# Batch 0 of an attention and MoE kernel: other key orders in two query chunks, earlier splits of the next z, and stores of empty rows behind a later block

## The chip, the core and the metric

The kernel runs on one core of one Trainium2 chip. The metric is the device time of one execution in microseconds (us), of which the median of several runs counts. The core has five engines that run their own instruction streams: PE (TensorE, matmuls), DVE (VectorE), ACT (ScalarE), POOL (GpSimd) and SP (SyncE, which here only issues DMAs). An instruction waits for others through semaphores, and all that stands behind a waiting instruction on its engine waits with it.

## The reference

First an attention without softmax over 8 batches of 1856 rows, then a mixture of 16 experts (4 groups of 4) over all 14848 rows; each row goes to the one expert that the logits choose.

```python
scores = scale * np.matmul(z, z.transpose(0, 2, 1))      # z: (8, 1856, 64), scale = 1/1856
attn = np.maximum(scores, 0.0) ** 2
out = np.matmul(attn, v)                                 # v: (8, 1856, 256)
x = (u * out).reshape(8 * 1856, 256)
...
g_idx = np.argmax(x @ w_group, axis=1)                   # then e_idx in that group
h = np.maximum(xg[mask_e] @ w1[g, e], 0.0)               # 256 -> 1024
out[tok_idx] = combined[:, None] * (h @ w2[g, e])        # 1024 -> 256
```

## The kernel before, in words

**Attention.** The queries of a batch are cut into four chunks (c = 0 to 3) of 512, 512, 512 and 320, the keys into 15 tiles of 128 (the last has 64). A step `s` is one (batch, chunk, i); `key(b, c, i)` says which key tile it takes, by the table `KORD` (in batch 0 chunk 0 simply `i`). A value is carried as a high and a low part, so a product is two or three matmuls. A step computes scores for one key tile (L371, L372: two matmuls into `sc`), ACT makes `r` of them (L375 relu, L382 square), DVE splits `r` into `ah` and `al` (L383, L386), and six matmuls (L409, tiles `o`) add it to the output: for each of two halves of the model dimension ah by vl, ah by vh, al by vh. Scores run six steps ahead of these products. The first scores of a chunk need `zm`, the chunk's queries, which in batch 0 and for (1, 0) DVE copies from the split z (L272, L273).

**Mirrored tiles.** The scores are symmetric. Where a key tile belongs to an earlier chunk's columns, its `r` has been transposed by DVE into a tile `mt` (L311), stored to DRAM by SP (`sym<-mt`, L319), and comes back as `at` (`at<-sym`, L327, in `load_mirror`, 12 or so steps ahead of its key); such a step has no score matmuls, only `ah`, `al` from `at` (L360, L361). In batch 0 these are keys 4 to 7 in chunk 2 and keys 4 to 11 in chunk 3.

**The next batch's inputs.** z and v of batch 1 are loaded and split during batch 0, at the steps that `PREP0` names: for each piece (chunk, i) of the load and (chunk, i) of the split. A split of z is an ACT cast `z2h` (L249) and a DVE subtraction `z2l` (L256) of the loaded `zr`; of v, `vh` and `vl` (L294, L295).

**Chunk end.** When a chunk's products are done, DVE multiplies them by u into `xT` (L431), ACT and DVE split that into `xh` and `xl` (L437, L442), PE makes the logits `pl` (L484, L485: four matmuls), SP transposes the rows (`rows<-pl`, L472). Rows that hold no token are stored from `padrow` into the experts' buckets (L979 for all experts during batch 0; L972 in `fill` later).

**Buffers.** `r`, `ah`, `al`, `mt`, `zr`, `z2h`, `z2l` all take turns in one pool of 31 buffers; `vr`, `vh`, `vl`, `xh`, `xl` in another of 18. A tile that takes a buffer waits for the last reader of what was in it, which can be a DMA. `zm` has 2 buffers, `at` 3, `y` 3.

**Order.** From step 15 on, PE, ACT and DVE run in the order in which the program is written; SP and POOL are ordered by the scheduler.

**Experts.** The first four experts are worked off in blocks 0 to 11 of gathered rows (`xp` loaded by SP, L784; `xf` L798, `xh_m` L803, `xl_m` L804; hidden products L819 to L821; `hh` L824, `hl` L830; second product L904; `yr` L917; `y` L943, L946 on DVE; POOL scatters y to the output, L947). After a block, `FILL` says for which experts the stores of 768 empty rows are issued by SP (L972). The other 12 experts follow in pairs, which the change leaves alone.

Of the kernel before, what the change touches and what calls it, by code (L numbers as in the profile page):

```python
# [29 lines left out]
def tile_glu_attn_moe(  # L30
# [307 lines left out]
    def key(b, c, i):  # L338
        if (b, c) == (B - 1, NQ - 1):
            return (0, 1, 12, 2, 3, 14, 4, 5, 13, 6, 7, 8, 9, 10, 11)[i]  # L340
        return KORD[c][i] if b or c else i

    NS = len(steps)
# [4 lines left out]
    def scores(s):  # L348
        b, c, i = steps[s]
        k = key(b, c, i)  # L350
        w = QW[b][c]
        for far in (ATL, 12):
            lb, lc, li = steps[min(s + far, NS - 1)]
            lk = key(lb, lc, li)
            if lk % KT == 0 and mirrored(lb, lc, lk) and ((lc, lk) == (3, 8) and lb < B - 1) == (far != ATL):
                load_mirror(lb, lk // KT, KB[lc])
# [37 lines left out]
    def attn_v(s):  # L394
        b, c, i = steps[s]
        k = key(b, c, i)
        vh, vl = bv[(b, k // 4)]
        if i == 0:
            oacc[s] = [bank(ps_o, "o", f"o_{b}_{c}_{d}") for d in range(ND)]
        oa = oacc[s - i]  # L400
        end = i == NK - 1
        ah, al = hl.pop(s)
        prods = [(d, q) for d in range(ND) for q in range(3 if al is not None else 2)]
        if s < 2:
            prods.sort(key=lambda x: x[1] == 2)
        held = pin if s < NK else same
        for d, q in prods:
            d0 = (k % 4) * D + d * P
            held(nc.tensor.matmul(  # L409
                oa[d][:, 0:QW[b][c]], (vh if q else vl)[:, d0:d0 + P], al if q == 2 else ah,  # L410
                start=(i == 0 and q == 0), stop=end and q == (1 if al is None else 2),
            ))
# [555 lines left out]
    def fill(j):  # L968
        regs(j)
        n = 512 if j >= NOLD else 768  # L970
        at = nc.sync.value_load(sti[0:1, j:j + 1], min_val=512, max_val=(NE - 1) * CAPB + N)
        nc.sync.dma_start(  # L972
            views[NMARK + j][ds(at, n), :].rearrange("(p t) w -> p t w", p=P),
            padrow.unsqueeze(1).to_broadcast([P, n // P, RW]),
        )
# [22 lines left out]
    if B == 1:  # L998
# [2 lines left out]

    prep = {}
    PREP0 = (
        ("v", 0, (0, 13), (1, 7)), ("v", 1, (1, 1), (1, 11)), ("v", 2, (1, 5), (1, 14)), ("v", 3, (2, 4), (3, 2)), ("z", 0, (2, 4), (3, 4)), ("z", 1, (2, 10), (3, 6)), ("z", 2, (3, 0), (3, 9)), ("z", 3, (3, 1), (3, 12)),
    )
    PREP = (
        ("v", 0, (0, 3), (0, 11)), ("v", 1, (2, 0), (2, 9)), ("v", 2, (2, 3), (2, 13)), ("v", 3, (2, 6), (2, 14)),
# [19 lines left out]
    for s in range(NS):  # L1027
        b, c, k = steps[s]
# [46 lines left out]
    def more_rows(i):  # L1075
        if not (deferred or gens):
            while late["loaded"] < min(NB, i + 2):
                load_rows(late["loaded"])
                late["loaded"] += 1
# [327 lines left out]
        return hs, [lambda g=g, m=m: step(g, m) for g, m in seq]  # L1407

    unsent = []
    FILL = {1: (0, 1), 2: (2, 3), 7: (4, 5)}  # L1410
    x = xs[0]
    for i, (e, r0, n) in enumerate(blocks):
        if i == 0:
# [38 lines left out]
        more_rows(i)  # L1452
        for j in FILL.get(i, ()):
            fill(j)
# [180 lines left out]
```

## Time and profile before

| | us |
|---|---|
| median of 3 runs | 1425.8 (1424.71 to 1426.95) |
| the profiled execution's own time | 1420.93 |
| its span, first to last instruction | 1419.2 |
| PE busy in it | 1407.8 (99%) |
| DVE busy | 1217.8 (86%) |
| ACT busy | 1046.3 (74%) |
| POOL busy | 435.9 (31%) |

The profiled execution is 4.87 us under the median of the runs; sums made against it are carried over to the median. The mean granted TensorE clock was 0.999. A time in the trace counts from the first instruction. In the timeline a row gives start, duration, engine, line, operation, output and inputs, and in brackets how long the engine was idle before it and what ended that. Ends of matmuls are modelled, and matmuls overlap in the pipeline, so their pace is read from start to start. On SP (shown as SPq) a row is the time that the issuing took, not the transfer.

### The profile page before, as it was taken

To read this page: it belongs to the slowest core of one execution; us is meant where nothing else is said; L and a number is where in the kernel's file an instruction comes from. 1 tells how busy PE (TensorE), PEld (TensorE's weight loads), DVE (VectorE), ACT (ScalarE), POOL (GpSimd) and SP (SyncE) were. 2 spreads that over 40 slices of the span, in tenths; PEclk is the share of its full clock that TensorE was granted. 3 is DMA by queue.
4 is the path that set the end of the run, shared out by engine and by line. 5 is a ranking of instruction groups with operands and counts; after the bars stand their busy time and mean duration, and the time that the engine had idled before them with its cause. 6 is when DMAs were issued, how large, how long until landed. Compare 5 with 4: busy or idle time off the path is not lost.

```text
span 1419.2 us, 22637 instructions
## 1 busy us (share of the span) xinstructions
PE 1407.8 (99%) x6986; PEld 1216.1 (86%) x6986; DVE 1217.8 (86%) x2433; ACT 1046.3 (74%) x1836; POOL 435.9 (31%) x460
## 2 busy tenths in 40 slices
PE   9999999999999999999999999999999999999998
PEld 7888888888888888888887898988888888899997
DVE  8989989899999999999988668789777788888884
ACT  8878787787877878878776354357777777777773
POOL 0002112220222112202223231332445555555554
PEclk9999999999999999999999999999999999999999
DMA  7888969989899799897976576635655555566652
GB/s 237 241 198 226 247 164 253 239 196 232 190 260 234 178 250 208 223 242 158 251 189 170 143 197 146 121 84 143 144 152 129 145 145 134 138 153 152 154 141 59
DMA packets 402411, 257.78 MB, mean 182 GB/s; under 512 B 243827, under 2 KB 356238, under 8 KB 402288
## 3 DMA queue, kind: packets, MB, share of 16 engines
q1 hardware_dynamic: 390384, 225.29, 65.6%
q0 software_dynamic: 11824, 30.90, 7.8%
q8 instruction: 55, 0.90, 0.3%
q14 instruction: 68, 0.56, 0.1%
q10 hardware_dynamic: 80, 0.13, 0.0%
HBM read 110.65 MB, written 88.33 MB: 140 GB/s over the span
## 4 chain that ended last, share of the span: by engine, by line
PE 88%; DVE 4%; issue 3%; DMA 3%; POOL 1%; ACT 1%; SPq 0%; POOLq 0%; DVEq 0%; ACTq 0%
PE o L409 38%; PE duo_p L904 15%; PE duo_y L1359 6%; PE sc L371 4%; PE sc L372 4%; PE yT L904 4%; PE duo_w L1359 2%; PE duo_x L1359 2%; PE duo_p L1359 2%; PE duo_z L1359 2%; PE ph L819 2%; PE ph L820 2%; PE ph L821 2%; DMA out_dram<-y_w,meta_w 1%; PE pl L485 1%
## 5 line engine op out<-in xcount | busy, mean ns | idle before, releaser
L409 PE MATMUL o<-ah,vl 128*128 128x512 f32 (+1 forms) x960 | 354.9, 370 | 0.5 <-DVE ah L383 0.4
L409 PE MATMUL o<-ah,vh 128*128 128x512 f32 (+1 forms) x960 | 354.4, 370 | 0.0
L409 PE MATMUL o<-al,vh 128*128 128x512 f32 (+1 forms) x896 | 328.8, 370 | 0.8 <-DVE al L361 0.8
L647 POOL DMA_INDIRECT bucket<-rows,di x120 | 133.8, 1115 | 386.0 <-issue 216.6
L375 ACT ACTIVATE r<-sc 128x512 f32<-128x512 f32 (+1 forms) x300 | 172.8, 576 | 79.7 <-PE sc L372 70.5
L409 PEld LDWEIGHTS o<-ah,vl 128*128 128x128 f32 x960 | 180.3, 188 | 32.2 <-DVE ah L383 1.1
L409 PEld LDWEIGHTS o<-ah,vh 128*128 128x128 f32 x960 | 180.3, 188 | 29.9
L947 POOL DMA_INDIRECT out_dram<-y_w,meta_w x92 | 139.1, 1512 | 190.4 <-ACT y_w L941 145.4
L386 DVE TENSOR_TENSOR al<-r,ah 128x512 fp32r<-128x512 f32 (+1 forms) x268 | 181.1, 676 | 15.9 <-DVE ah L383 0.5
L409 PEld LDWEIGHTS o<-al,vh 128*128 128x128 f32 x896 | 167.9, 188 | 28.3 <-DVE al L361 1.1
L904 PE MATMUL duo_p<-hh_w,duo_w 128*128 128x496 f32 (+10 forms) x692 | 177.9, 371 | 0.0
L382 ACT ACTIVATE r<-r 128x512 f32<-128x512 f32 (+1 forms) x266 | 163.8, 616 | 8.5
L904 PEld LDWEIGHTS duo_p<-hh_w,duo_w 128*128 128x128 f32 x692 | 128.6, 188 | 16.7
L383 DVE CAST ah<-r 128x512 fp32r<-128x512 f32 (+1 forms) x266 | 110.4, 415 | 18.8 <-ACT r L382 9.8
L371 PE MATMUL sc<-zm,z2h 128*128 128x512 f32 (+1 forms) x300 | 116.2, 387 | 1.5 <-DVE zm L273 0.9
L372 PE MATMUL sc<-zm,z2l 128*128 128x512 f32 (+1 forms) x300 | 114.9, 383 | 0.0
L311 DVE STREAM_TRANSPOSE mt<-r 128x512 f32<-128x512 f32 x157 | 110.8, 706 | 0.7
L904 PE MATMUL duo_p<-hl_w,duo_w 128*128 128x496 f32 (+10 forms) x346 | 104.2, 371 | 0.0
L361 DVE TENSOR_TENSOR al<-at,ah 128x512 fp32r<-128x512 f32 (+1 forms) x180 | 101.8, 578 | 2.7 <-ACT ah L360 2.6
L360 ACT CAST ah<-at 128x512 fp32r<-128x512 f32 (+1 forms) x180 | 91.8, 530 | 5.9 <-DMA at<-sym 3.1
L824 ACT ACTIVATE hh<-ph 128x512 fp32r<-128x512 f32 (+6 forms) x96 | 45.4, 487 | 39.6 <-PE ph L821 38.9
L904 PE MATMUL yT<-hh,w_e 128*128 128x512 f32 (+6 forms) x352 | 73.9, 328 | 0.0
(263 smaller groups left out, 2876.1 us busy)
## 6 DMA issues: line engine op xcount, KB each, us to landing
sym<-mt SPq DMA_DIRECT2D x134, 256.0 KB
duo_r<-in_w_dram SPq DMA_DIRECT2D x48, 512.0 KB
at<-sym SPq DMA_DIRECT2D x88, 256.0 KB
bucket<-padrow SPq DMA_DIRECT2D x28, 528.0 KB
at<-sym SPq DMA_DIRECT2D x92, 160.0 KB
ut<-in_uT_dram SPq DMA_DIRECT2D x24, 512.0 KB
vr<-in_v_dram SPq DMA_DIRECT2D x23, 512.0 KB
raw_e<-in_w_dram SPq DMA_DIRECT2D x16, 512.0 KB
```

Source lines behind the costliest of these rows:

```text
L311: nc.vector.transpose(out=t2.rearrange("p (j t x) -> p t j x", t=KT, x=32), in_=a.rearrange("p (t j x) -> p t j x", t=KT, x=32))
L371: held(nc.tensor.matmul(ps[:, 0:w], z2h[:, ks], zm, start=True, stop=False))
L372: held(nc.tensor.matmul(ps[:, 0:w], z2l[:, ks], zm, start=False, stop=True))
L375: held(nc.scalar.activation(out=a, in_=ps[:, 0:w], func=AF.Relu, scale=1.0 / S))
L382: held(nc.scalar.activation(out=a, in_=a, func=AF.Square))
L383: held(nc.vector.tensor_copy(out=ah, in_=a))
L386: held(nc.vector.tensor_sub(out=al, in0=a, in1=f32(ah)))
L409: held(nc.tensor.matmul(oa[d][:, 0:QW[b][c]], (vh if q else vl)[:, d0:d0 + P], al if q == 2 else ah, start=(i == 0 and q == 0), stop=end a ...
L647: nc.gpsimd.indirect_dma_start(out=views[(b * NQ + 2 * half + hs[h]) * NT + i], out_offset=bass.IndirectOffsetOnAxis(ap=di[0:n, i0 + i:i0 ...
L904: nc.tensor.matmul(o, wt["2"][f // 2][:, w0:w0 + P], hs[f][q // 2][:, c0:c0 + n], start=(at == 0), stop=(at == 3 * NF - 1))
L947: nc.gpsimd.indirect_dma_start(out=outs(), out_offset=bass.IndirectOffsetOnAxis(ap=meta[0:m, t, 1:2], axis=0), in_=y[0:m], in_offset=None, ...
L1359: nc.tensor.matmul(out, a, b, start=(q == 0 and m in (1, 5)), stop=(q == 2), skip_group_check=True)
```

## The change

Two lines are added in `key`, and two tables of numbers change. In batch 0 the third chunk (c = 2) and the fourth (c = 3) get key orders of their own, in which the mirrored keys are spread differently among the others. The loads and splits of batch 1's four z pieces move earlier. The stores of empty rows for the experts 2 and 3 go from behind block 2 to behind block 5. Line numbers behind L341 rise by 2 in the changed kernel.

```diff
     def key(b, c, i):
...
+        if b == 0 and c > 1:
+            return ((12, 0, 4, 13, 1, 14, 5, 2, 3, 6, 8, 9, 7, 10, 11), (0, 4, 1, 5, 2, 6, 12, 7, 3, 13, 14, 8, 9, 10, 11))[c - 2][i]
         return KORD[c][i] if b or c else i
...
     PREP0 = (
-        ... ("z", 0, (2, 4), (3, 4)), ("z", 1, (2, 10), (3, 6)), ("z", 2, (3, 0), (3, 9)), ("z", 3, (3, 1), (3, 12)),
+        ... ("z", 0, (1, 12), (2, 5)), ("z", 1, (2, 4), (2, 11)), ("z", 2, (2, 8), (3, 4)), ("z", 3, (2, 9), (3, 9)),
     )
...
-    FILL = {1: (0, 1), 2: (2, 3), 7: (4, 5)}
+    FILL = {1: (0, 1), 5: (2, 3), 7: (4, 5)}
```

Before, batch 0 used `KORD[2] = (12, 0, 13, 1, 14, 2, 8, 3, 9, 4, 10, 5, 11, 6, 7)` and `KORD[3] = (0, 1, 2, 3, 12, 4, 5, 6, 7, 13, 14, 8, 9, 10, 11)`.

**Where the rows of chunk 1 are transposed (SP).** The third chunk's last two mirrored stores (`sym_0_2_3<-mt_0_2_13` and `..._14`) stand there among stores of empty rows (`bucket<-padrow`) and loads. The kernel before:

```order
L472 DMA_TRANSPOSE rows_0_0_548<-pl_0_0_550 128x4x128 x4
L319 DMA sym_0_2_3_756<-mt_0_2_13_806 128x512
L979 DMA bucket_69<-padrow_70 512x1x264
L319 DMA sym_0_2_3_756<-mt_0_2_14_841 64x512
L979 DMA bucket_69<-padrow_70 512x1x264 x2
```

The changed kernel:

```order
L474 DMA_TRANSPOSE rows_0_0_548<-pl_0_0_550 128x4x128 x4
L981 DMA bucket_69<-padrow_70 512x1x264
L244 DMA zr_1_0_807<-in_zT_dram 128x512
L319 DMA sym_0_2_3_761<-mt_0_2_13_819 128x512
L981 DMA bucket_69<-padrow_70 512x1x264
L319 DMA sym_0_2_3_761<-mt_0_2_14_856 64x512
L981 DMA bucket_69<-padrow_70 512x1x264
```

One store of empty rows and the load of `zr_1_0` now stand ahead of the store of `mt_0_2_13`.

**What waits for that store (ACT, and behind it DVE).** On ACT in the kernel before, `r_40` takes the buffer of `mt_0_2_13` and waits for its store:

```order
L375 ACTIVATE r_38_918<-sc_38_915 128x512
L382 ACTIVATE r_38_918<-r_38_918 128x512
L360 CAST ah_39_935<-at_0_1_2_791 128x512
L375 ACTIVATE r_40_952<-sc_40_949 128x512
L382 ACTIVATE r_40_952<-r_40_952 128x512
```

In the changed kernel `z2h_1_0` takes that buffer, and stands behind `r_40` (ACT):

```order
L377 ACTIVATE r_40_947<-sc_40_944 128x512
L384 ACTIVATE r_40_947<-r_40_947 128x512
L249 CAST z2h_1_0_960<-zr_1_0_807 128x512
L377 ACTIVATE r_41_970<-sc_41_967 128x512
L384 ACTIVATE r_41_970<-r_41_970 128x512
```

On DVE of the changed kernel `z2l_1_0` of this cast stands between `al_40` and the fourth chunk's `zm_0_3`:

```order
L385 CAST ah_40_949<-r_40_947 128x512
L388 TENSOR_TENSOR al_40_952<-r_40_947,ah_40_949 128x512
L256 TENSOR_TENSOR z2l_1_0_961<-zr_1_0_807,z2h_1_0_960 128x512
L272 CAST zm_0_3_964<-z2h_0_3_305 64x320
L273 CAST zm_0_3_964<-z2l_0_3_306 64x320
```

So the copies into `zm_0_3` now stand behind the split of z that waits for the store.

**The last products ahead of batch 1's first scores (PE).** `sc_60` is the first score of batch 1; `xl_0_2`, which the logits and a chain on DVE need, takes the buffer of a v piece that a product of chunk 3 reads last. In the kernel before that is `vl_0_0`, read last by step 48, five steps of products ahead of the logits:

```order
L409 MATMUL o_0_3_1_1142<-ah_48_1090,vl_0_0_186 128x320
L409 MATMUL o_0_3_1_1142<-ah_48_1090,vh_0_0_185 128x320
L409 MATMUL o_0_3_1_1142<-al_48_1093,vh_0_0_185 128x320
L371 MATMUL sc_55_1221<-zm_0_3_963,z2h_0_3_305 128x320
L372 MATMUL sc_55_1221<-zm_0_3_963,z2l_0_3_306 128x320
```

In the changed kernel it is `vl_0_1` (keys 4 to 7), read last by step 52, whose key is 7:

```order
L411 MATMUL o_0_3_1_1146<-ah_52_1153,vl_0_1_257 128x320
L411 MATMUL o_0_3_1_1146<-ah_52_1153,vh_0_1_256 128x320
L411 MATMUL o_0_3_1_1146<-al_52_1154,vh_0_1_256 128x320
L411 MATMUL o_0_3_0_1145<-ah_53_1180,vl_0_0_186 128x320
L411 MATMUL o_0_3_0_1145<-ah_53_1180,vh_0_0_185 128x320
L411 MATMUL o_0_3_0_1145<-al_53_1183,vh_0_0_185 128x320
L411 MATMUL o_0_3_1_1146<-ah_53_1180,vl_0_0_186 128x320
L411 MATMUL o_0_3_1_1146<-ah_53_1180,vh_0_0_185 128x320
L411 MATMUL o_0_3_1_1146<-al_53_1183,vh_0_0_185 128x320
L486 MATMUL pl_0_2_1298<-xh_0_2_1163,whl_85 48x512
L487 MATMUL pl_0_2_1298<-xl_0_2_1164,wh0_86 48x512
```

Behind these come the other two logits and `sc_60`. Between the last read of that buffer and `sc_60` there now stand eight products (two of step 52, six of step 53) and four logits on PE; before, these were two products of step 48, two scores, the steps 49 to 53 and four logits. On DVE, fifteen instructions from the first `xl_0_2` to the second `zm_1_0` stand there before as after, the same but for `z2l_1_2` in place of `z2l_1_0`.

## Rows read from the trace of the kernel before

**Rows 1.** The page: busy time of each engine, share of the span, instructions.

```profile
PE 1407.8 (99%) x6986; PEld 1216.1 (86%) x6986; DVE 1217.8 (86%) x2433; ACT 1046.3 (74%) x1836; POOL 435.9 (31%) x460
```

**Rows 2.** Timeline of PE, 79 to 80.4 us: start, duration, instruction, idle before it.

```profile
79.02 0.39 PE L409 MATMUL o<-ah,vh 128*128 128x512 f32 x1
79.25 0.39 PE L409 MATMUL o<-al,vh 128*128 128x512 f32 x1
80.14 0.38 PE L371 MATMUL sc<-zm,z2h 128*128 128x320 f32 x1 [0.51 <-DVE zm L273]
```

**Rows 3.** Timeline of SP's DMA issues, 62 to 92 us.

```profile
67.17 6.23 SPq L472 DMA_TRANSPOSE rows<-pl  x4
73.50 0.52 SPq L319 DMA_DIRECT2D sym<-mt  x1
74.08 1.06 SPq L979 DMA_DIRECT2D bucket<-padrow  x1
...
84.57 0.63 SPq L244 DMA_DIRECT2D zr<-in_zT_dram  x1
```

**Rows 4.** The chain of waits, 66 to 80.6 us: start, length, what.

```profile
75.27 3.65 DMA sym<-mt
```

**Rows 5.** Timelines of ACT and of DVE, 76 to 80 us.

```profile
76.91 0.60 ACT L375 ACTIVATE r<-sc 128x512 f32<-128x512 f32 x1 [5.15 <-PE pl L485]
...
79.67 0.32 DVE L273 CAST zm<-z2l 64x320 fp32r<-64x320 f32 x1
```

**Rows 6.** Timeline of PE, 93 to 100 us.

```profile
93.29 0.31 PE L409 MATMUL o<-ah,vl 128*128 128x320 f32 x1
...
98.42 0.40 PE L484 MATMUL pl<-xh,whl 128*48 128x512 f32 x1
...
99.12 0.39 PE L485 MATMUL pl<-xl,wh 128*48 128x512 f32 x1
99.87 0.47 PE L371 MATMUL sc<-zm,z2h 128*128 128x512 f32 x1 [0.36 <-DVE zm L273]
```

**Rows 7.** Timeline of DVE, 93 to 100 us.

```profile
93.68 1.29 DVE L442 TENSOR_TENSOR xl<-xT,xh 128x512 fp32r<-128x512 f32 x2
...
96.82 0.69 DVE L256 TENSOR_TENSOR z2l<-zr,z2h 128x512 fp32r<-128x512 f32 x1
```

**Rows 8.** Timelines of SP and of DVE, 809 to 843 us.

```profile
813.89 1.34 SPq L972 DMA_DIRECT2D bucket<-padrow  x2
820.66 1.28 SPq L784 DMA_TRANSPOSE xp<-bucket  x1
...
820.87 0.46 DVE L943 COPY y<-yr 128x512 uint16<-128x512 uint16 x1 [2.75 <-DMA out_dram<-y,meta]
```

**Rows 9.** Timeline of PE, 820 to 844 us.

```profile
820.97 0.31 PE L821 MATMUL ph<-xl_m,w1h_e 128*128 128x320 f32 x1
822.17 0.41 PE L819 MATMUL ph<-xh_m,w1l_e 128*128 128x320 f32 x1 [0.89 <-DVE hl L830]
...
842.47 0.28 PE L904 MATMUL yT<-hl,w_e 128*128 128x256 f32 x1
843.07 0.43 PE L819 MATMUL ph<-xh_m,w1l_e 128*128 128x368 f32 x1 [0.33 <-ACT xh_m L803]
```

**Rows 10.** Timelines of ACT, SP and DVE, 842 to 860 us.

```profile
842.21 0.81 ACT L803 CAST xh_m<-xf 128x736 fp32r<-128x736 f32 x1 [2.63 <-DVE xf L798]
...
842.41 1.23 SPq L784 DMA_TRANSPOSE xp<-bucket  x1
...
859.43 0.76 DVE L798 COPY xf<-xp 128x1024 uint16<-128x1024 uint16 x1
```

**Rows 11.** PE's last and first matmuls; one stretch, granted clock in its third-last column.

```profile
1412.85 0.28 PE L858 MATMUL py_w<-duo_w,h_w 128*128 128x256 f32 x1
...
1417.00:1418.00 1.00, 0.00 (x0) 0.00 (x0) 0.00 (x0) 0.00 (x0) 0.00 (x0) 0.88 0.05 14
...
1.31 3.98 PE L990 MATMUL warm_ps<-ones 128*128 128x128 bf16 x40 [1.31 <-POOL ones L131]
```

More of the change, by code (lines that the diff above doesn't have):

```diff
@@ L1003, in tile_glu_attn_moe @@
     PREP0 = (
-        ("v", 0, (0, 13), (1, 7)), ("v", 1, (1, 1), (1, 11)), ("v", 2, (1, 5), (1, 14)), ("v", 3, (2, 4), (3, 2)), ("z", 0, (2, 4), (3, 4)), ("z", 1, (2, 10), (3, 6)), ("z", 2, (3, 0), (3, 9)), ("z", 3, (3, 1), (3, 12)),
+        ("v", 0, (0, 13), (1, 7)), ("v", 1, (1, 1), (1, 11)), ("v", 2, (1, 5), (1, 14)), ("v", 3, (2, 4), (3, 2)), ("z", 0, (1, 12), (2, 5)), ("z", 1, (2, 4), (2, 11)), ("z", 2, (2, 8), (3, 4)), ("z", 3, (2, 9), (3, 9)),
     )
```

## The prediction

> **What bounds the kernel now.** I read the page first. PE is busy 1407.8 us, 99% of the span [rows 1]. The reader should see that no engine's total can be shortened into a gain: the other three have room, and the change takes no matmul away and adds none. The time can move only through the moments in which PE stands still. So I next looked in the list of waits and in PE's timeline for those moments near the places that the change touches. There are four, and each is measured from start to start, since ends are modelled. I call a stall what the next matmul starts later than the pace allows.
>
> - Stall A, 79 us. Products of 512 columns follow each other at 0.23 us (79.02 to 79.25), which by columns makes 0.144 for 320 and 0.115 for 256; so the first score of chunk 3 was due at 79.48 and came at 80.14: 0.66 us, waiting for DVE's copy into `zm_0_3` [rows 2].
> - Stall B, 99 us. Logits start from 98.42 to 99.12 at (99.12 - 98.42)/3 = 0.233 us; `sc_60` was due at 99.35 and came at 99.87: 0.52 us, waiting for DVE's copy into `zm_1_0` [rows 6].
> - Stall C, 821 us. By the pace for 320 columns due at 821.11, came at 822.17: 1.06 us, waiting for `hl` [rows 9].
> - Stall D, 842 us. By the pace for 256 columns due at 842.59, came at 843.07: 0.48 us, waiting for `xh_m` [rows 9].
>
> Together 2.72 us. That is all that the change could take away at these places, and it is 0.19% of the time. About 0.2% (2.85 us) is what a measurement of this kernel can tell from no change. So even a perfect outcome would hardly show as faster; the question is what the change adds.
>
> **Part 1: the order around 79 us.** In the kernel before, SP issues four transposes of rows until 67.17 + 6.23 = 73.40, then the store of `mt_0_2_13` at 73.50 [rows 3]. ACT's `r_40`, which takes that tile's buffer, starts at 76.91 after 5.15 us of idle time [rows 5]. The bracket names the logits, of which nothing is an input of `r_40`; by the buffer that it takes I read it as the store's landing, some 3.4 us after its issue. The chain of waits has the same for the next store: issued at 75.27, landed 3.65 us later [rows 4].
>
> After the change a store of empty rows and the load of `zr_1_0` stand ahead of this store. From the rows: the store of empty rows costs SP 1.19 (from 74.08 to the issue of the next at 75.27), the load 0.63 and about 0.1 to the next [rows 3, 4]. The issue moves from 73.50 to 73.50 + 1.19 + 0.73 = 75.42, and with 3.65 the landing to 79.07. The waiting instruction is now ACT's `z2h_1_0`. Then in line: the cast, about 0.6 with its start (an ACT row of that width takes 0.60 [rows 5]) to 79.75; DVE's `z2l_1_0`, 0.69 alone [rows 7], 0.6 to the next start, to 80.4; two copies of 0.32 into `zm_0_3` [rows 5] to 81.05; 0.14 to PE. The score starts near 81.2 where 79.48 was due: a stall of 1.72 in place of 0.66, **+1.06**. `r_40` itself is no longer held, and `r_41` and all else on ACT behind the cast wait; the products that need them come after the score.
>
> Bounds: if the store landed as early as before, the same line would end at 78.95, and the stall would vanish: -0.66. If the two transfers ahead of it cost not the 1.92 of their issues but twice that, because their data has to go through first, another 1.92 comes on top: +2.98. I take 1.06, because the pair of stores in [rows 3, 4] is the nearest case: one store of empty rows ahead of a mirrored store, in the same queue, 2 us away.
>
> **Part 2: the order around 99 us.** In the kernel before, the chain on DVE from `xl_0_2` (93.68) to the score (99.87) took 6.19 us [rows 6, 7]; fifteen DVE instructions stand there back to back. It began 0.39 after the start of the product at 93.29, which is the last reader of the buffer that `xl_0_2` takes [rows 6, 7]. PE had more than 6 us of work from that product on, so only 0.52 was lost.
>
> In the changed order the last reader is a product of step 52 instead. PE has from its start: itself and eight more products of 320 columns, 9 x 0.144 = 1.30, and four logits, 4 x 0.233 = 0.93, in sum 2.23, before `sc_60`. DVE's fifteen instructions are as many as before, with another split of z of equal size, so 0.39 + 6.19 = 6.58 from the same start. The stall is 6.58 - 2.23 = 4.35 in place of 0.52: **+3.83**.
>
> Bounds: if the buffer came from elsewhere, or DVE had done half its chain earlier, the stall could be gone: -0.52. If one of the chain's ACT inputs (`z2h_1_2`, `r_55`) came late, the chain grows by up to an ACT instruction, 0.6: +4.4. I take 3.83, since the order of the fifteen is fixed and they ran without a pause.
>
> Such an idle time is far longer than any of PE in these rows (0.89 [rows 9]), so TensorE's clock has to be looked at. The one long idle time of the trace is its end: PE's last matmul starts at 1412.85 and takes 0.28, and the granted clock falls only in the microsecond from 1417, whose mean is 0.88 between the levels 1.00 and 0.50 (2.4 and 1.2 GHz) [rows 11]. Before that it had been held through almost four microseconds of nothing. So I add nothing to the sum. The Trainium skill (TensorE: Matmul & The Clock Gate, section "Part 1: The HAM clock gate") says that the slow clock is the default, which activity lifts and an idle array gets back. The fall at the end agrees with that; by this rule the clock might fall already near 100 us, and the sum would be that of rival 3.
>
> **Part 3: stores of empty rows behind block 5.** SP issues two stores from 813.89, and its next issue, a load from the same buckets, comes only at 820.66 [rows 8]. Meanwhile DVE's `y` waits 2.75 us for a buffer that the scatter of an earlier y still holds, until 820.87 [rows 8], and `hl` behind it gives stall C. Everything that SP issues afterwards is late by the same wait, ACT's `xh_m` at the end of it (2.63 idle before it) [rows 10], which is stall D. Behind block 5 the scatter finds no such stores in its way at 818, and SP goes on some 5 us earlier: **-1.06 and -0.48**, bounds 0 for each. The stores' new place lies on SP ahead of the load of `xp_7`, which was issued at 842.41 and first used at 859.43 [rows 10]: 17 us of cover against 6.8 us, the time from the stores' issue to SP's next one. If that cover were gone, up to about 1 us, a stall like C, would come back.
>
> **Sum.** +1.06 + 3.83 - 1.06 - 0.48 = +3.35 on the profiled execution: 1420.93 becomes 1424.3. On the median, 1425.8 + 3.3 = **1429.1**. The rest of the change (loads of z sooner, key orders as such) only moves work on DVE and ACT that lies beside PE's, with 14% and 26% of room [rows 1].
>
> **Rivals.**
> 1. The spread does what its shape suggests: the splits of z and of mirrored tiles are out of the way, and A to D all vanish. Sum -2.72, **1423.1**. For it: A and B both wait for DVE's copies [rows 2, 6], and the change moves splits of z on DVE. Against: the store's place on SP and step 52 as last reader follow from the written order. It decides if `z2h_1_0` and `xl_0_2` start without waiting.
> 2. Only one of the stalls grows. If A stays at 0.66, -1.54 + 3.83 = +2.3, 1428.1; if B stays at 0.52, -1.54 + 1.06 = -0.5, 1425.3. For the latter: DVE was busy up to the start of `xl_0_2` in the kernel before, so that the trace does not show a wait for that buffer itself.
> 3. Stall B is long enough to lose the clock. At the start 40 matmuls of 128 columns take 3.98 us [rows 11], where 40 x 0.23/4 = 2.3 would be full pace: a return from the low level costs about 1.7 us, an estimate from these two. 3.35 + 1.7 = +5.0, **1430.8**. Decided by whether the granted clock falls at all near 100 us.
> 4. The change's third part does nothing since stalls C and D move with the stores: +4.9, 1430.7.
>
> **How the numbers follow.** Forecast as worked out (own range 1428.0 to 1430.5): 0.54, of which I count 0.12 under the bound of 2.85, since +3.35 lies near it. Rival 1: 0.14, of which 0.06 comes out faster by over 0.2% through the spread of the runs and 0.08 within. Rival 2: 0.18, within. Rivals 3 and 4: 0.10 and 0.04, slower. Slower 0.42 + 0.14 = 0.56, within 0.2% 0.12 + 0.08 + 0.18 = 0.38, faster 0.06. The range leaves out rival 1 and takes in the rest: 1425.0 to 1431.2.
>
> **What would show it.** Right: PE idle for about 4 us ahead of the score near 100 us with DVE `zm` L273 as releaser, about 1.6 us near 80 us, and none at the places of C and D; on ACT a long idle time ahead of `z2h_1_0`; granted clock 1.00 behind 100 us. Wrong: PE's waits in batch 0 under 1 us in all, which would be rival 1; `xl_0_2` starting on DVE without a wait (rival 2); 512-column products at double pace behind 100 us (rival 3); a stall near 840 to 860 us (rival 4).

## The result and the profile after

The changed kernel took 1434.66 us (median of 6 runs, 1430.44 to 1437.76), the kernel before on the same chip 1425.43 (6 runs). The medians lie 9.2 us apart; the ratio of the runs, by which this document goes, is 1.0052, with an interval of 1.0035 to 1.0068: **slower by 7.4 us** (5.0 to 9.7). The forecast was +3.3, and 1434.66 lies above the range. The profiled execution took 1435.77, with a span of 1434.0 and a mean granted clock of 0.997.

The page's first line, which answers to [rows 1], again has PE at 99%:

```profile
PE 1413.3 (99%) x6986; PEld 1217.1 (85%) x6986; DVE 1218.0 (85%) x2433; ACT 1041.6 (73%) x1836; POOL 435.4 (30%) x460
```

The timeline of PE at the places of [rows 2] (stall A) and [rows 6] (stall B):

```profile
79.19 0.39 PE L411 MATMUL o<-al,vh 128*128 128x512 f32 x1
81.56 0.38 PE L373 MATMUL sc<-zm,z2h 128*128 128x320 f32 x1 [1.98 <-DVE zm L273]
...
99.53 0.31 PE L411 MATMUL o<-ah,vh 128*128 128x320 f32 x1
99.67 0.31 PE L411 MATMUL o<-al,vh 128*128 128x320 f32 x1
...
100.52 0.39 PE L487 MATMUL pl<-xl,wh 128*48 128x512 f32 x1
105.04 0.76 PE L373 MATMUL sc<-zm,z2h 128*128 128x512 f32 x1 [4.13 <-DVE zm L273]
...
106.03 0.47 PE L411 MATMUL o<-ah,vl 128*128 128x320 f32 x1
106.29 0.47 PE L411 MATMUL o<-ah,vh 128*128 128x320 f32 x1
```

From start to start, A is 81.56 - 79.19 - 0.23 = 2.14 us (forecast 1.72), and B is 105.04 - 100.52 - 0.23 = 4.29 (forecast 4.35). The last two rows hold what was not forecast: products of 320 columns start 0.26 apart, where they had been 0.14 to 0.15 apart before the stall (99.53, 99.67). The windows of the same stretch say why; the granted clock stands third from the end:

```profile
102.00:104.00 2.00, 0.00 (x0) 0.00 (x0) 1.90 (x6) 0.58 (x2) 0.00 (x0) 0.99 0.46 93
104.00:106.00 2.00, 0.96 (x2) 0.83 (x3) 1.92 (x7) 0.00 (x0) 0.00 (x0) 0.50 0.54 115
106.00:108.00 2.00, 2.00 (x8) 1.93 (x7) 1.97 (x8) 1.70 (x3) 0.00 (x0) 0.50 0.39 88
108.00:110.00 2.00, 2.00 (x8) 1.75 (x7) 0.81 (x2) 1.64 (x3) 0.00 (x0) 0.50 0.13 26
110.00:112.00 2.00, 2.00 (x11) 1.81 (x10) 1.80 (x4) 1.23 (x2) 0.20 (x1) 0.80 0.15 26
```

The clock fell to the low level (1.2 GHz) while PE stood still and came back some 6 us after it had resumed. If half of the busy time is lost at half clock, that is 0.5 x (0.96 + 2 + 2) + 0.2 x 2 = 2.9 us. Such a sum (one minus the clock, times PE's busy time) is called "lost to the clock" below. It is an estimate on the high side: by the pace of the products (0.26 for 0.147) a little under half is lost.

What PE waited for, on SP, ACT and DVE (timelines; they answer to [rows 3, 5, 7]):

```profile
72.56 0.57 SPq L244 DMA_DIRECT2D zr<-in_zT_dram  x1
73.26 0.85 SPq L319 DMA_DIRECT2D sym<-mt  x1
...
79.51 0.62 ACT L249 CAST z2h<-zr 128x512 fp32r<-128x512 f32 x1 [7.05 <-DMA sym<-mt]
...
80.16 0.69 DVE L256 TENSOR_TENSOR z2l<-zr,z2h 128x512 fp32r<-128x512 f32 x1 [5.31 <-ACT z2h L249]
...
88.90 0.62 ACT L249 CAST z2h<-zr 128x512 fp32r<-128x512 f32 x1 [0.82 <-DMA zr<-in_zT_dram]
...
89.55 0.69 DVE L256 TENSOR_TENSOR z2l<-zr,z2h 128x512 fp32r<-128x512 f32 x1 [0.95 <-ACT z2h L249]
...
98.85 1.29 DVE L444 TENSOR_TENSOR xl<-xT,xh 128x512 fp32r<-128x512 f32 x2 [1.08 <-PE o L411]
...
104.47 0.42 DVE L273 CAST zm<-z2l 64x512 fp32r<-64x512 f32 x1
```

The first four rows are the chain of A as forecast: the store of the mirrored tile behind the load of `zr_1_0`, ACT's cast waiting for that store, DVE behind it. `xl_0_2` waits for a product on PE, as forecast for B. Two rows were in no step of the prediction: at 88.90 the cast of the next z piece waits for the landing of its own load, and DVE stands behind it.

Stalls C and D [rows 9] are gone from this trace, but it has a longer wait near their place, on PE's timeline:

```profile
814.97 0.44 PE L821 MATMUL ph<-xh_m,w1l_e 128*128 128x384 f32 x1 [2.49 <-ACT xh_m L805]
```

Neither can simply be put down to the moved stores. Three kernels of the experiments that keep the stores behind block 2 (`FILL` as before, the z pieces alone, piece 1 alone) show no C and no D either, and the key orders alone show a part of C (0.53 us). And a wait for `xh_m` of 1.8 to 2.7 us near 802 to 827 us stands in all seven later profiles from chips on which the kernel before took 1426 us or more, and in none of the eleven from those on which it took 1419 us; the second profile of the changed kernel (the first experiment) is one of the eleven. All eight kernels that show it have the moved stores, and the one profile of the kernel before (1420.93) is 4.5 us under its median here, so whether the stores have a part in it stays open.

### The profile page after: what moved, and what is told of

It reads as the page before. It is cut to its first block, busy times and chain, and to the rows that moved or that the text cites. A ratio compares the mean times of both kernels' runs of the same rounds, so it can differ in the third digit from the quotient of the medians.

```text
span 1434.0 us, 22624 instructions
## 1 busy us (share of the span) xinstructions
PE 1413.3 (99%) x6986; PEld 1217.1 (85%) x6986; DVE 1218.0 (85%) x2433; ACT 1041.6 (73%) x1836; POOL 435.4 (30%) x460
## 4 chain that ended last, share of the span: by engine, by line
PE 82%; DVE 6%; DMA 4%; issue 3%; ACT 2%; SPq 2%; POOL 1%; DVEq 0%; POOLq 0%; ACTq 0%
PE o L411 33%; PE duo_p L906 14%; PE duo_y L1361 6%; PE yT L906 5%; PE sc L373 4%; PE sc L374 4%; PE duo_x L1361 2%; PE duo_w L1361 2%; PE ph L823 2%; PE ph L821 2%; PE ph L822 2%; PE duo_p L1361 2%; PE duo_z L1361 2%; DMA zr<-in_zT_dram 1%; DMA out_dram<-y_w,meta_w 1%
```

## The experiments

Each kernel was run in turns with the kernel before on one chip, and its ratio is taken there; the kernel before took medians of 1418.8 to 1427.5 on these chips.

**1. The changed kernel once more, and its parts.** First the changed kernel without any edit:

> The changed kernel once more, on the chip of the next three. Theory: +0.4 to +0.6% against before (about +7 us), the waits near 80 and 100 us at about 2 and 4.3 us and the clock at 0.50 behind the second; the waits of the first trace behind 280 us, which no later run had, are not part of it and are gone. Rival: they belong to the changed kernel and are here again, with a time above +9 us.

Measured: 1.0056 (1.0043 to 1.0069). PE's timeline and two windows:

```profile
79.38 0.39 PE L411 MATMUL o<-al,vh 128*128 128x512 f32 x1
82.35 0.39 PE L373 MATMUL sc<-zm,z2h 128*128 128x320 f32 x1 [2.58 <-DVE zm L273]
...
101.31 0.39 PE L487 MATMUL pl<-xl,wh 128*48 128x512 f32 x1
105.82 0.76 PE L373 MATMUL sc<-zm,z2h 128*128 128x512 f32 x1 [4.12 <-DVE zm L273]
```

```profile
106.00:108.00 2.00, 2.00 (x7) 1.81 (x8) 1.93 (x9) 0.92 (x2) 0.00 (x0) 0.50 0.68 149
108.00:110.00 2.00, 2.00 (x11) 1.81 (x10) 1.59 (x4) 1.87 (x4) 0.00 (x0) 0.78 0.12 27
```

A is 2.74, B 4.28, and 1.5 us were lost to the clock. The stores of empty rows alone:

```diff
-    FILL = {1: (0, 1), 2: (2, 3), 7: (4, 5)}
+    FILL = {1: (0, 1), 5: (2, 3), 7: (4, 5)}
```

> The kernel before with only the third part of the change (stores of empty rows for the experts 2 and 3 behind block 5). Theory (the loss comes from batch 0): between no change and -1.5 us against before, and the waits of 1.06 us before hl and 0.48 us before xh_m in the blocks 2 to 4 are gone. Rival (the moved stores cost by themselves what the changed kernel showed near its blocks 1 to 3, a wait of 2.65 us for xh_m): +1.5 us or more, with that wait in its trace.

Measured: 0.9993 (0.9984 to 1.0002). PE has no wait at all between 800 and 860 us. What the stores are worth, -1.0 us (-2.3 to +0.3), cannot be told from nothing. The rest of the change without it (`FILL` as before):

> The changed kernel with the stores of empty rows back behind block 2 (key orders and z splits alone). Theory: the waits near 80 and 100 us as in the changed kernel (2.1 and 4.3 us against 0.67 and 0.52 before), the granted clock at 0.50 for some 6 us after the second, which costs 2.8 us more; in sum about +8 us against before, and the waits of 1.06 and 0.48 us in the blocks 2 to 4 are back. Rival (the moved stores make a part of the loss): +6.5 us or less.

Measured: 1.0052 (1.0038 to 1.0066); A 1.80, B 4.29, 1.5 us lost to the clock. The loss is that of batch 0. C and D, which the theory expected back, are not there: this trace too has no wait between 800 and 860 us, so their absence from the one above says nothing of the stores. Within batch 0, the two key orders alone (old `PREP0`, old `FILL`):

> The kernel before with the two new key orders of batch 0 alone (old z loads and splits, stores of empty rows behind block 2). Theory (the earlier z loads and splits make the loss: the split of z0 waits for a late transfer near 72 to 79 us, DVE stands still meanwhile and is late by that in all that follows): the wait near 80 us is at most 1 us, that near 100 us at most 1 us, granted clock 1.00, time within 1.5 us of before. Rival (key 7 late in the fourth chunk frees the buffer of xl_0_2 too late): the wait near 100 us is above 3 us, the clock falls, +5 us or more.

Measured: 1.0001 (0.9992 to 1.001); A 0, B 1.46 (a wait of 1.30), clock 1.00. In this program `xl_0_2` starts at 93.80 without a wait for PE, ahead of key 7's products (from about 96.4): it takes another buffer. And the loads and splits of z alone (old `key`, old `FILL`):

> The kernel before with the earlier z loads and splits alone (old key orders, stores behind block 2). Theory (as in kord_only): the wait near 80 us is 1.5 to 2.5 us, that near 100 us about 3 us, the clock falls behind it, +4 to +6 us. Rival (key orders make the loss): both waits as before (0.67 and 0.52), within 1.5 us of before.

Measured: 1.004 (1.0027 to 1.0053). The wait of A has moved to the logits at 78 us (1.57), B is 2.28, the clock, expected to fall, stays at 1.00; its profiled run (1422.23) is 2.3 us under its median of 1424.57, so this profile doesn't show the whole loss. What follows: the key orders by themselves cost nothing that shows, the earlier z pieces do.

**2. The clock.** Sixteen matmuls with no use ahead of `sc_60` keep PE busy during B:

```diff
+        for _ in range(16 if s == 60 else 0):
+            nc.tensor.matmul(ps[:, 0:512], z2h[:, ks], z2h[:, 0:512], start=True, stop=True)
         held(nc.tensor.matmul(ps[:, 0:w], z2h[:, ks], zm, start=True, stop=False))
```

> The changed kernel with 16 extra matmuls of 512 columns on PE directly ahead of the first score of batch 1, into the bank that this score then starts anew; they take 3.7 us and lie inside the 4.3 us in which PE waits there. Theory (the clock falls because PE stands still): the first score starts as late as in the changed kernel, but the granted clock stays at 1.00 behind it and the time falls by about 2.8 us against the changed kernel, to +5.2 us against before. Rival (the clock falls for another reason or costs nothing): granted clock 0.50 near 105 us again, or no change against the changed kernel.

Measured: 1.0039 (1.0025 to 1.0053). PE's timeline, and two windows:

```profile
101.35 3.79 PE L374 MATMUL sc<-z2h 128*128 128x512 f32 x16
105.70 0.50 PE L375 MATMUL sc<-zm,z2h 128*128 128x512 f32 x1 [0.56 <-DVE zm L273]
```

```profile
100.00:104.00 4.00, 4.00 (x20) 3.18 (x20) 3.86 (x11) 3.97 (x10) 0.00 (x0) 1.00 0.56 36
104.00:108.00 4.00, 3.44 (x19) 2.73 (x18) 3.82 (x15) 1.76 (x4) 0.00 (x0) 1.00 0.50 99
```

`sc_60` comes as late as before, but the clock stays at 1.00: in the trace the 1.5 to 2.9 us lost at the low level are gone. What that gives in time is not clear of the noise. The ratio is 0.0013 and 0.0017 (1.9 and 2.4 us) below the two of the changed kernel, with overlapping intervals, and the kernel with `FILL` as before took only 1.1 us more on the same chip (1426.82, against 1425.77).

**3. Key 7, and the place of the copies.** The fourth chunk in its old key order:

```diff
-        if b == 0 and c > 1:
+        if b == 0 and c == 2:
```

> The changed kernel with the fourth chunk's old key order in batch 0. Theory (the long wait before the first score of batch 1 comes from the place of key 7, the last reader of the buffer that xl_0_2 takes): that wait falls from 4.3 us to 0.5 or less, the granted clock stays at 1.00, and the time falls by 3.8 + 2.8 = 6.6 us against the changed kernel, to about +2.6 us against before; the wait near 80 us stays at about 2.1 us. Rival (the earlier z splits hold DVE, whatever the order): the wait stays above 3 us and the clock falls again.

Measured: 1.0032 (1.0021 to 1.0043); A 2.10, B still 3.06, and the clock fell here too (1.7 us lost). `xl_0_2` no longer waits for PE, but DVE reaches it only at 97.84, in place of 93.68 [rows 7], with no pause right ahead of it. So the buffer of key 7 is not the whole cause of B. Next, the copies into `zm_0_3` and `zm_1_0` behind the second key of their chunk:

```diff
-        if k == (5 if s < NK else 5) and nxt < B * NQ:
+        if k == (1 if nxt in (3, 4) else 5) and nxt < B * NQ:
```

> The changed kernel with DVE's two copies into zm_0_3 and into zm_1_0 four steps earlier in DVE's order, each ahead of the instructions that wait. Theory (the two long waits of PE are these copies standing behind waiting instructions): both waits ahead of the first scores are gone, at most about 1 us comes up in their place (logits or products waiting for xl or al), the granted clock stays at 1.00, and the time is between -2 and +1 us against before. Rival (DVE as a whole is late): other waits of 3 us or more take their place near 80 or 100 us and the time stays above +4 us.

Measured: 1.0022 (1.0012 to 1.0031). No score waits for `zm` any more and the clock stays at 1.00, but PE still loses 0.67 us at 80 us, where a score waits for ACT, and 0.80 us at a product near 103 us: ACT and DVE are late whatever stands there. The time, +3.1 us (1.7 to 4.4), lies between the theory's and the rival's.

**4. Piece 0 of z: four kernels that did not settle it.** First its split later, then also the old fourth chunk (the edit of experiment 3):

```diff
-        ("z", 0, (1, 12), (2, 5)),
+        ("z", 0, (1, 12), (3, 3)),
```

> The changed kernel with the split of the next z piece 0 moved from step (2,5) to (3,3); its load stays early. Theory (the split that stands ahead of zm_0_3 makes stall A, the buffer read last by the product of key 7 makes stall B): A falls to 0.7 us or less, B stays at 4.3 us or grows to 4.9, since one more split stands in DVE's chain, the clock falls behind it; about 1.0040 of the time before. Rival (B comes from DVE being late since the wait at 75 us): without that wait DVE reaches xl in time, B falls to 3 us or less, perhaps without a fall of the clock; about 1.002.

> The same, and the fourth chunk in its old key order, so that neither the early split of z nor key 7 is left. Theory (two causes of stall B, DVE's lateness and the buffer; both are gone): A 0.7 us or less, B 1.5 or less, granted clock 1.00 behind it, 1.0000 to 1.0010 of the time before. Rival (the earlier loads on SP, or the other z splits, cost by themselves): B or new waits of 2 us and more stay, 1.002 or more.

Measured: 1.0036 (1.0022 to 1.005) with A 0.50, B 5.02; and 1.0045 (1.0032 to 1.0059) with A 0.87, B 4.11. The first went as its theory had it. The second did not: neither the early split of piece 0 nor key 7 is left in it, and B is as long as ever. Its rival, the earlier loads or the other splits, was right and gave the lead. Then piece 0 loaded and split as before the change, with the new orders and with the old fourth chunk:

```diff
-        ("z", 0, (1, 12), (2, 5)), ("z", 1, (2, 4), (2, 11)), ("z", 2, (2, 8), (3, 4)),
+        ("z", 0, (2, 4), (3, 4)), ("z", 1, (2, 4), (2, 11)), ("z", 2, (2, 8), (3, 5)),
```

> The changed kernel with z piece 0 loaded at step (2,4) and split at (3,4), as before the change (and z piece 2 split one step later, at (3,5)); key orders, the other pieces and the stores of empty rows as in the changed kernel. Then nothing on ACT near 80 us takes the buffer of a mirrored tile whose store is late. Theory (DVE has no slack between 80 and 100 us; it restarts late because of that store and carries 1.2 us more of z splits): it restarts in time, so that only the splits are left: A 0.3 us or less, B at most 2 us, clock 1.00, 1.0000 to 1.0015 of the time before. Rival (the buffer that xl_0_2 takes, read last by the product of key 7, makes B by itself): B 4 us or more, the clock falls, 1.003 or more.

> The same with the fourth chunk in its old key order. Theory: as the kernel above, B at most 2 us, 0.9995 to 1.0015. Rival (buffer of key 7): the only one of the two with B small, 1.0005 or less against 1.003 or more above. Rival (the earlier loads of the other z pieces cost by themselves): both 1.002 or more.

Measured: 1.0024 (1.001 to 1.0038) with A 0, B 5.01; and 1.0035 (1.0021 to 1.0049) with A 0, B 4.77. The theory (the late mirrored store) fell: A is gone with it, B is not. The timelines of ACT and PE of the first of the two show what had been there all the time:

```profile
88.25 0.62 ACT L249 CAST z2h<-zr 128x512 fp32r<-128x512 f32 x1 [3.93 <-DMA zr<-in_zT_dram]
...
103.78 0.77 PE L373 MATMUL sc<-zm,z2h 128*128 128x512 f32 x1 [4.84 <-DVE zm L273]
```

ACT stands 3.93 us until the load of z piece 1 has landed. In every kernel with the split of piece 1 at (2,11) this cast starts between 88.2 and 90.7 us, whatever came earlier, and where the copies keep their place the second copy into `zm_1_0` ends 13.8 to 15.3 us behind the start of its `z2l`.

**5. Piece 1 of z.** It alone, in the kernel before:

```diff
-        ("z", 1, (2, 10), (3, 6)),
+        ("z", 1, (2, 4), (2, 11)),
```

> The kernel before with one edit: z piece 1 loaded at (2,4) and split at (2,11), as in the changed kernel; piece 0, key orders and stores of empty rows as before. Theory (that split is written ahead of the landing of its own load, near 88 us in every kernel that has it; ACT and DVE stand until then, and DVE needs 14 us from there to the second zm_1_0 copy): DVE idle 3 us ahead of the z2l at 89 us, the second zm_1_0 copy ends at 102.5 to 103.5, B 3.5 to 4.5, the clock falls, 1.002 to 1.0045 of the time before. Rival (it needs key 7 or the late mirrored store as well): B 1.5 us or less, 1.0010 or less.

Measured: 1.0046 (1.0032 to 1.0059): within the intervals, one entry of a table makes a loss as large as that of the whole change. SP's, ACT's, DVE's and PE's timelines:

```profile
78.05 2.68 SPq L327 DMA_DIRECT2D at<-sym  x4
...
81.85 0.85 SPq L244 DMA_DIRECT2D zr<-in_zT_dram  x2
...
89.45 0.62 ACT L249 CAST z2h<-zr 128x512 fp32r<-128x512 f32 x1 [4.66 <-DMA zr<-in_zT_dram]
...
90.11 0.69 DVE L256 TENSOR_TENSOR z2l<-zr,z2h 128x512 fp32r<-128x512 f32 x1 [4.36 <-ACT z2h L249]
...
104.09 0.77 PE L371 MATMUL sc<-zm,z2h 128*128 128x512 f32 x1 [4.25 <-DVE zm L273]
```

The load is written at (2,4) but issued only at 81.85, behind the mirrored loads that stand ahead of it on SP; it has landed by 89.45. The new entry brought the issue only some 2 us sooner (84.57 [rows 3]), while the split moved ten steps ahead. B is 4.40, 0.8 us more is lost at a product near 91 us, and 3.0 to the clock. Now the changed kernel with that split moved back:

```diff
-        ("z", 1, (2, 4), (2, 11)),
+        ("z", 1, (2, 4), (3, 6)),
```

> The changed kernel with the split of z piece 1 moved back to (3,6); its load stays early. Theory of two floors under sc_60 (DVE 14 us behind the landing of piece 1, and the buffer that the product of key 7 frees): the first is gone and the second stays, so A 2 us, B 3.6 to 4.3, xl_0_2 waiting visibly for PE by 1.5 us or more, the clock falls, 1.003 to 1.005 of the time before. Rival (the landing alone): B 1.0 to 2.2, clock 1.00, 1.0005 to 1.0025.

Measured: 1.0045 (1.0031 to 1.0059); A 1.92, B 4.27, 2.7 us lost to the clock. DVE's and PE's timelines:

```profile
98.33 1.30 DVE L444 TENSOR_TENSOR xl<-xT,xh 128x512 fp32r<-128x512 f32 x2 [2.56 <-PE o L411]
...
104.50 0.76 PE L373 MATMUL sc<-zm,z2h 128*128 128x512 f32 x1 [4.11 <-DVE zm L273]
```

DVE now stands 2.56 us for key 7's product, and B is as long as it was: this is the prediction's mechanism without the landing. The rest of B, some 1.7 us, is DVE's lateness from A. The same with the old fourth chunk (the edit of experiment 3):

> The same with the fourth chunk in its old key order: both floors gone, z piece 0 still split ahead of zm_0_3. Theory: A 1.8 to 2.7 stays, B 1.0 to 2.2 (DVE restarts 2 us late behind the mirrored store and has one split more than in the kernel before, PE has lost the 2 us of A), clock 1.00, 1.0005 to 1.0020 of the time before. Rival (the late mirrored store keeps B at 3 us by itself): clock falls, 1.003 or more.

Measured: 1.0016 (1.0007 to 1.0025). B is 0.40, smaller than expected, because PE itself came later; and the clock fell behind A, which was in neither theory. DVE's copies into `zm_1_0` still end only at 103.08, where they had ended at 99.72 in the kernel before. PE's and DVE's timelines and a window:

```profile
81.96 0.38 PE L373 MATMUL sc<-zm,z2h 128*128 128x320 f32 x1 [2.11 <-DVE zm L273]
...
102.51 0.39 PE L487 MATMUL pl<-xl,wh 128*48 128x512 f32 x1
103.14 0.50 PE L373 MATMUL sc<-zm,z2h 128*128 128x512 f32 x1 [0.24 <-DVE zm L273]
...
102.66 0.42 DVE L273 CAST zm<-z2l 64x512 fp32r<-64x512 f32 x1
```

```profile
82.00:84.00 2.00, 2.00 (x6) 1.71 (x7) 1.93 (x5) 1.97 (x4) 0.00 (x0) 0.56 0.50 148
```

So B has **two causes, either of which holds it at 3 to 5 us without the other**, and of two floors under one instruction the later one counts. (Key 7 does so only beside the earlier z pieces; with the key orders alone `xl_0_2` takes another buffer.) The 0.4 that is left without both makes it look better than it is: PE's last logit starts at 102.51 in place of 99.12 [rows 6], and of that 1.7 us are the clock lost behind A. Without that loss B would be about 2.1 (0.40 + 1.7, an estimate). That is a third, lower floor: DVE restarts late behind A and has one split more. The time agrees: without both causes the ratio is 1.0016, with key 7 alone 1.0045, and with piece 1 alone 1.0032 (the last two intervals, to 1.0025 and from 1.0021, just overlap).

**6. A version that beats both.** The kernel before with the stores behind block 5 and the copies into `zm_0_3` four steps sooner; then also `zm_1_0` three steps sooner, with the split that it needs:

```diff
-        if k == (5 if s < NK else 5) and nxt < B * NQ:
+        if k == (1 if nxt == 3 else 2 if nxt == 4 else 5) and nxt < B * NQ:
...
-        ("z", 0, (2, 4), (3, 4)),
+        ("z", 0, (2, 4), (3, 1)),
```

(the first of the two has `1 if nxt == 3 else 5` and the old split).

> The kernel before with the stores of empty rows behind block 5, and the fourth chunk's queries zm_0_3 copied four steps sooner (behind the second key of chunk 2). Theory (stall A of the kernel before is the wait for zm_0_3, which stands late on DVE): A gone, B 0.5 as before, 0.9988 to 0.9995 of the time before. Rival (the copies only delay other work on DVE by as much): B or another wait grows by the 0.6 us of the copies, 0.9993 or more.

> The same, and the first copies for batch 1, zm_1_0, three steps sooner too, with the split of z that they need at (3,1) instead of (3,4). Theory: A and B both gone, 0.9985 to 0.9992 of the time before. Rival (the earlier split puts a wait ahead of the fourth chunk's first steps, as in the changed kernel): a wait of 0.5 us or more near 80 us, 0.9993 or more.

Measured: 0.9988 (0.9979 to 0.9997) with A 0 and B 0.67, and **0.9983 (0.9974 to 0.9992)**, -2.4 us (-3.7 to -1.1), with A and B at 0. In the second DVE copies `zm_1_0` at 93.20, and PE goes on without a wait; the next score then waits 0.30 us for its own z split:

```profile
93.20 0.41 DVE L272 CAST zm<-z2h 64x512 fp32r<-64x512 f32 x1
...
98.47 0.40 PE L373 MATMUL sc<-zm,z2h 128*128 128x512 f32 x1
...
100.52 0.50 PE L374 MATMUL sc<-zm,z2l 128*128 128x512 f32 x1 [0.30 <-DVE z2l L256]
```

What of this the earlier copies give is not shown: the stores alone gave 0.9993 (0.9984 to 1.0002), and all three intervals overlap; in that trace A was 0.19 without any earlier copy, so that A differs by execution. The second's trace still has a wait of 2.36 us for `xh_m` at 802 us, with the clock at 0.50 behind it.

The same early copy of `zm_1_0` with the new key orders (stores behind block 5, old z loads, z piece 0 split at (3,1), `zm_0_3` not copied sooner):

> The new key orders and the stores behind block 5, the z loads as before the change, z piece 0 split at (3,1) and zm_1_0 copied behind the third key of chunk 3. Theory (of the change the key orders are harmless, and B is only the place of zm_1_0 on DVE): A and B gone, 0.9980 to 0.9992 of the time before, level with the kernel that has the early copies and the old orders. Rival (the new orders cost where DVE is late): a wait of 1 us or more near 100 us, 0.9995 or more.

Measured: 1.0002 (0.999 to 1.0014). The rival was right: that wait for `z2l` is 2.24 us here, and 1.7 us more are lost to the clock behind it. With the orders of before it is 0.30.

## Why the prediction was wrong, point by point

**The reading of the bound** held: no engine's total moved the time, and the four places A to D were those that the change touched.

**Part 1, stall A: right mechanism, a little too small.** The term was +1.06; measured against 0.66 before it was +1.48, and +1.14 (`FILL` as before) and +2.08 (changed, again) in the two kernels of experiment 1 that have all of batch 0's change. The step "the issue moves from 73.50 to 75.42 and with 3.65 the landing to 79.07" came near the cast's start (79.51) by two errors of opposite sign. The issue was no later than before in this trace (73.26; 73.84 and 75.00 in the two others); it was the landing that took longer, 79.51 - 73.26 = 6.25 us to its user (5.16 and 5.30 in the others) where it had been 3.41 [rows 3, 5]. Two transfers stood ahead of it in the queue, a store of empty rows and the load of z; that they made the landing later was the prediction's bound, and no run moves them alone.

**Part 2, stall B: right to 0.06 us, and still not the whole cause.** The term was +3.83; measured 4.29 - 0.52 = +3.77. The kernel with piece 1's split moved back shows the forecast chain by itself. What was missed is that the split of piece 1 holds DVE back by nearly as much: `xl_0_2` waits for key 7's product only 1.08, 0.41 and 0.65 us in the first three traces with all of batch 0's change, and not at all in the one with the sixteen matmuls. The sentence "the rest of the change (loads of z sooner, key orders as such) only moves work on DVE and ACT that lies beside PE's, with 14% and 26% of room" is false for one entry of the table: alone it costs 0.46%. Room over the span says nothing of an instruction that stands for a load; I had followed the wait of piece 0's cast and had not asked when the load of piece 1 is issued. It did not spoil the sum, since the two floors don't add.

**The clock: this step failed.** "So I add nothing to the sum." The rows at the program's end show one idle time and one fall [rows 11]: by its mean of 0.88 the clock fell near 1417.8, some 4.6 us behind the last matmul. That is 0.3 us more than the 4.35 forecast for B, and one fall does not show that a shorter idle time is safe. It fell in both traces of the changed kernel, which lost 2.9 and 1.5 us by it. The Trainium skill (TensorE: Matmul & The Clock Gate, section "Part 1: The HAM clock gate") has an idle array return to the slow clock, and the trace agrees: 0.50 from 104 us. Rival 3 had the right mechanism, and a chance of 0.10, which was far too low. That its price of 1.7 us lies between 1.5 and 2.9 is luck: it was read from the 40 matmuls at the start, where the profile shows the granted clock at 1.00 throughout (1 to 6 us).

**Part 3: not shown.** C and D are gone from the trace, as forecast (-1.54), but three traces with the stores in their old place lack them too, and the stores alone gave -1.0 (-2.3 to +0.3). The term took one execution's waits for a lasting cost.

**The sum with measured terms**: in the first trace of the changed kernel A +1.5, B +3.8, clock +2.9, together +8.2, or +6.6 if C and D (-1.5) count; in the second +2.1, +3.8 and +1.5, together +7.3 or +5.8. Measured +7.4 (5.0 to 9.7), and +7.9 (6.1 to 9.8) in the second comparison. So of the 4.1 us between forecast and result, the clock, put at nothing, makes 1.5 to 2.9, stall A 0.4 to 1.0, and the gain of 1.5 at C and D is doubtful. The same balance for the kernels that move these terms, A and B of the kernel before (1.2) taken off, and 1.0, as measured for the stores alone, where they are behind block 5; the waits near 802 to 827 us are left out:

| kernel | A | B | lost to the clock | balance | measured, us |
|---|---|---|---|---|---|
| changed, again | 2.7 | 4.3 | 1.5 | +6.3 | +7.9 (6.1 to 9.8) |
| old fourth chunk | 2.1 | 3.1 | 1.7 | +4.7 | +4.5 (3.0 to 6.1) |
| key orders alone | 0 | 1.5 | 0 | +0.3 | +0.1 (-1.1 to 1.4) |
| piece 1 alone | 0.8 (at 91 us) | 4.4 | 3.0 | +7.0 | +6.5 (4.5 to 8.4) |
| piece 1's split back | 1.9 | 4.3 | 2.7 | +6.7 | +6.4 (4.4 to 8.4) |
| both causes gone | 2.3 | 0.4 | 1.7 | +2.2 | +2.3 (1.0 to 3.5) |
| piece 0 as before | 0 | 5.0 | 3.0 | +5.8 | +3.4 (1.4 to 5.4) |

The last row lies outside by 0.4 us. Two kernels that are not in the table lie outside the other way, and further: the earlier z pieces alone (+2.8 for +5.7, 3.8 to 7.5) and the early copies of experiment 3 (-0.7 for +3.1, 1.7 to 4.4). Their profiled runs are 2.3 and 1.6 us under their medians, which suggests waits in their other runs; no trace here shows them, so that part of these two losses stays unexplained.

**The rivals.** Rival 1 (all four stalls vanish) and rival 2 (one of them grows) fell: both A and B grew. Rival 4 (C and D move with the stores) stays open: where the moved stores go with a wait for `xh_m`, the kernel before was not profiled, and where they go with none, C and D are mostly absent without them too.

## What to carry to other kernels

Before a load and its use are moved earlier in the written order, look up when the queue will issue that load and what stands ahead of it there; an engine that reaches the use first stands still, and everything behind it is late by the same amount, however much room its total shows. Where undoing one part leaves a wait as long as it was, look for a second cause that sets the same instruction, and undo both. A stall of PE has to be priced with the clock that it may lose, here 1.5 to 3.0 us on top of waits of 2 to 5 us. A wait that one execution shows is not yet a wait of the kernel: see it in a second trace before it gets a term in a sum.

## What the runs showed of the hardware

- How long PE stood still did not alone decide whether the granted clock fell: it fell with waits of 2.11 us (at 82 us, old fourth chunk and piece 1's split back) and 2.24 us (new key orders with the early copies), and did not fall with 2.58 us (at 82 us, changed kernel again) and 2.12 us (at 103 us, earlier z pieces alone). What else decides is open. In two kernels (the old fourth chunk, alone and with piece 0's split later) it fell only 1.2 to 1.5 us after PE had gone on. Once low, it stayed so for 3 to 7 us, with PE at work again for most of them.
- With sixteen matmuls whose result nobody reads in a wait of 4.3 us, 3.8 us of it filled, it stayed at 1.00.
- A store to DRAM behind a store of empty rows and a load of z took 5.0 to 6.3 us from its issue to its user on ACT in nine profiles and 3.9 in a tenth, where it took 3.4 to 4.7 in four profiles without them. No run moves these two transfers alone.
